# Other constants for a kernel's build-time scheduler: urgencies of loads and attention, a first chunk of eleven tiles, exponentials gathered in fours, loads expected at 290 GB/s

## The chip, the cores and the metric

The kernel runs on one core of a Trainium2 chip. The time is the device time of that core in microseconds. Engines are named as in the profile: PE (TensorE), DVE (VectorE), ACT (ScalarE), POOL (GpSimd), and SP (SyncE), whose queue issues most of the DMAs.

## The reference

Three stages follow each other. Attention works on 4 batches of 8 heads, 576 tokens, head dimension 64: one softmax attention over means of four neighbouring tokens (`out_d`, repeated four times along the sequence), plus one that sees only keys less than four positions away. The two sums make a matrix of 2304 tokens x 512. Then come two dense blocks, with all of their weights in float64, which the kernel reads as 64-bit words:

```python
def _moe_ref(x, w_in, w_out):            # 2304 x 512, d_ff 2048
    h = x @ w_in
    g = h * np.cos(h)
    return (g @ w_out).astype(np.float32)

def _moe2_ref(x, w1, w2, w3, w_out):     # 2304 x 512, d_ff 1024
    a = x @ w1
    b = x @ w2
    h = a * b @ w3
    return (h @ w_out).astype(np.float32)
```

## The kernel before

**Weights.** Each 128x512 block of 64-bit words is loaded on SP's queue into a tile `raw` and turned into float32 by `w_job` (L308): ACT writes `t`, DVE shifts `t` (TENSOR_SCALAR), DVE joins both words (SCALAR_TENSOR_TENSOR). For `wi` (of `w_in`) and `wo` (of `w_out`) ACT then copies a rounded part and POOL subtracts it, so that each product is made of three matmuls of rounded parts (`mm3`). `w3` and `w4` (of the second block's `w3` and `w_out`) are multiplied with each other beforehand, in plain float32: `w5_job` (L733) makes 64 calls into four banks `ps_w`, in two rounds of 32. `w5_out_job` (L755) copies each of the four banks to a slot of kind `t` and stores it from ACT's queue (`w_sc<-w`); the slot counts as free only when the store has landed (`give_stored`, L239), and six slots of kind `t` serve everything that is converted.

**Attention.** A pair of heads (`pair_job`, L446) goes through scores `ps_s`, exponentials `sd`, a division, transposes `ps_t`, copies `ptp`, product `ps_p`, and ACT's copy `up`. A unit of 192 tokens (`unit_job`, L571) goes through `ps_sb`, `sc`, the exponential, sums `bsum`, POOL's product, transposes `ps_tb` with copies `pt` on ACT, and `ps_av`; DVE adds both parts to `xb`, ACT and POOL split it into `xs`. Two units make a chunk of 384 tokens, and six chunks make the whole. Pooled values take `vr` and `vd` on DVE.

**First dense block.** A step is one chunk by one of 32 tiles of 128 hidden units. `h_job` (L826) makes 12 matmuls into a bank `ps_h`; `chain_job` (L806) makes g = h cos(h) of it: `turns` on ACT, `c` on DVE, Sin and Square on ACT, `c` on DVE (this gives the bank back), then `g` on ACT and POOL. `y_job` (L853) makes the 12 matmuls into four banks `ps_y` that stay open for the chunk; at a hand-over to other tokens `y_out_job` (L877) copies them to `yt` on ACT and stores them. `plan` (L783) sets the order: chunk 0 runs over the first HALF tiles, chunk 1 over the same tiles, then both over the rest, then the other chunks over all 32. The sums of the first part go to `part_sc`. The second dense block (`ps_ab`, `ps_o`) follows at 582 us.

**What sets the order.** All of these are jobs of a scheduler that runs while the program is built. Its own clock goes by `cost` (L83) and by the delays in LATENCY (L62). Whenever an engine is free by that clock, the ready job with the lowest urgency gets it (`run`, L264), so constants shift whole rows of instructions on every engine; on the chip each engine then works its row off in that order and waits only on semaphores. Urgencies of loads and attention come from A0, A1 and the U_ constants (L55 to L58, used in L1074 to L1115): the jobs of chunk 0 have A0 plus U_QK, U_PAIR, U_POOL or U_UNIT, the converters of `w4` and `w3` -1 to 7, those of the second round of `w3` 8 + U_W3 and on, those of `wi` and `wo` 16 + U_WI or U_WO plus the tile's first step, each step of h and its chain 16 plus its number. Copies of `ps_w` have -20, those of `ps_y` -10. SLACK (L53) is how long a slot must have been free before a load may go into it. `exps` (L552) holds exponentials until TOGETHER of them wait, or the first has waited for PATIENCE ns, or ACT's table is that of Exp anyway, so that it is swapped with Sin less often. While PE has nothing to do before the first h step, `warm_up` fills in matmuls on zeros (`ps_z`, or into `ps_w`).

Of the kernel before, what the change touches and what calls it, by code (L numbers as in the profile page):

```python
# [13 lines left out]
I64 = mybir.dt.int64  # L14
# [29 lines left out]
NH = N2 // 2  # L44
NCH2 = NT // N2
NQ = 7
HALF = 10
SCALE = 1.0 / math.sqrt(D)
TWO_PI = 2.0 * math.pi
LAG = 3  # L50
WARM = 256
EARLY_WARM, RISEN, REST = 3000.0, 10000.0, 130.0
FIRST, SLACK = 3000.0, 1000.0  # L53
TOGETHER, PATIENCE = 3, 6000.0
A0, A1 = 11, 4  # L55

U_QK, U_PAIR, U_POOL, U_UNIT = -13, -12, -11.5, -8
U_WI, U_WO, U_W3 = -4, -0.5, -1  # L58
OUT_BANKS = (4, 5, 6, 7, 2, 3)
EARLY = 2  # L60
BIAS, BANDS = 2, 4
LATENCY = {"pe": 200, "se": 140, "ve": 130, "ge": 150, "sy": 2000}  # L62


def band_of(u, w):
# [5 lines left out]
def fused_kernel(ctx: ExitStack, tc: tile.TileContext, qk_block, v_block, qk_pool, v_pool,  # L71
# [8 lines left out]
    def size(a):  # L80
        return math.prod(a.shape[1:])

    def cost(name, op, out, ins, func):  # L83
        n = max(size(a) for a in [out] + ins)
        if name == "ve":
            shared = n > 64 and ends["ge"] > max(now[0], ends["ve"])
            if op.startswith("tensor_scalar") and len(ins) == 1:
                return 90 + n * (1.5 if shared else 0.65)
            both = len(ins) == 2 and n > 64 and not any(a.tensor.name.startswith("ps_") for a in ins)
            return 75 + n * (2.2 if both and shared else 1.17 if both else 1.04)  # L90
        if name == "se":
            load = 1283 if func in (AF.Exp, AF.Sin) and func != table[0] else 0
            table[0] = func if load else table[0]
            return (60 if ins[0].tensor.name.startswith("ps_") else 100) + n / 1.2 + load
        if name == "ge":
            return 160 + (1.7 if any(0 in [step for step, _ in a.ap] for a in ins) else 2.3) * n
        if name == "sy":
            return max(450, n * out.shape[0] * (8 if out.dtype == I64 else 4) / 310)
        n = size(out)
        if op == "transpose":  # L100
            return 70
        if ins[0].dtype == F32R:
            return 12.5 + n / 2.4
        return (4 if ins[0].shape[0] == P else 2) * max(35, n / 2.4)

    def visible(a):

        end, by = written.get(a.tensor.name, (0.0, "pe"))
        return end + LATENCY[by]

    class Engine:
# [3 lines left out]
        def __getattr__(self, op):  # L115
            call = getattr(self.engine, op)

            def issue(*args, **kw):
                also = kw.get("accum_out")
                aps = [a for a in list(kw.values()) + list(args) if isinstance(a, bass.AP) and a is not also]  # L120
                out = kw["out"] if "out" in kw else args[0]
                if op == "dma_start" and self.name != "sy":
                    ends[self.name] = max(now[0], ends[self.name]) + 70
                    written[out.tensor.name] = ends[self.name] + cost("sy", op, out, [out], None), "sy"
                    return call(*args, **kw)
                first = next(k for k, a in enumerate(aps) if a is out)
                ins = aps[:first] + aps[first + 1:]
                end = ends[self.name] = max(now[0], ends[self.name]) + cost(self.name, op, out, ins, kw.get("func")) + (0 if also is None else 183)
                for a in (out, out if also is None else also):
                    written[a.tensor.name] = end, self.name  # L130
                return call(*args, **kw)  # L131

            return issue

    ve, se, pe, ge, sy = (Engine(*e) for e in (("ve", nc.vector), ("se", nc.scalar), ("pe", nc.tensor), ("ge", nc.gpsimd), ("sy", nc.sync)))
# [71 lines left out]
    def until(cond):  # L207
        while not cond():
            yield "until", cond
# [26 lines left out]
    def give(name, slot, engine):  # L236
        free[name].append((ends[engine] + LATENCY[engine], slot))

# [7 lines left out]
    def reached(key, n):  # L246
        return lambda: done.get(key, 0) >= n
# [535 lines left out]
    def plan():  # L783

        f = 0
        while f < F1:
            if f >= HALF:
                yield from until(lambda: reached(("x", 1), UPC)() or ("wi", f) in w_t)
# [260 lines left out]
    with tc.manual_schedule():  # L1049
# [20 lines left out]
        first, seen = {}, []  # L1070
        first.update({i: HALF if i == 1 else F1 * i for i in range(NC1)})
        first.update({("f", f): f if f < HALF else f + HALF for f in range(F1)})

        def attention(i, at):  # L1074

            for b in sorted({(UPC * i + m) // UPB for m in range(UPC)} - set(seen)):
                seen.append(b)
                if b < EARLY:
                    for m in range(UPB):
                        Job(at + U_QK + 0.5 * m, unit_qk_job(UPB * b + m))  # L1080
                for p in range(KC):
                    Job(at + U_PAIR + 2 * p, pair_job(b, p))
                    Job(at + U_POOL + 2 * p, pool_v_job(b, p))
            for m in range(UPC):
                Job(at + U_UNIT + 3 * m, unit_job(UPC * i + m))
# [24 lines left out]
        for i in range(2, NC1):  # L1110
            run(reached("h", first[i - 1] + 1 if i > 2 else first[0] + HALF + 1))
            attention(i, W5 + first[i])
# [71 lines left out]
```

## Time and profile before

| | |
|---|---|
| median of 3 runs | 866.26 us (864.69 to 868.79) |
| the profiled execution | 865.21 us |
| its span in the trace | 863.4 us |
| PE busy | 842.7 us, 98% |
| DVE, ACT, POOL busy | 503.3, 446.9, 366.6 us (58%, 52%, 42%) |
| HBM traffic | 89.49 MB read, 27.79 MB written |
| the chain that ended last | PE 86%, DVE 5%, DMA 4%, ACT 2% of the span |

PE is nearly always busy, so a term of time is either a stretch in which PE waits, or one in which it runs at half clock: the clock granted is half in two short stretches, one that ends 16.3 us after the start and one near 112 to 118.6 us. Nearly every operation is recorded by one helper line, L131 (DMA issues of ACT: L125), so the tiles' names tell the operations apart.

### The profile page before, as it was taken

The page shows a single profiled execution, that of the slowest core. Times are in us where ns is not written, and L with a number is a line of the kernel's source. Part 1 is how long each engine was busy: PE and PEld are TensorE (multiplying, and loading weights), DVE is VectorE, ACT ScalarE, POOL GpSimd, SP SyncE. Part 2 cuts the span into 40 slices and gives each one's busy share as a digit, 9 for nine tenths or more (in the row PEclk, how much of TensorE's full clock was granted, in tenths as well). Part 3 has the DMA queues.
Part 4 walks back from the last instruction along what each step waited for, and adds up shares of the span by engine and source line. Part 5 has one row for each costly group of instructions (what it writes and reads, how often), then busy time and mean ns, then how long its engine had stood idle before and what let it go on. Part 6 is the DMA issues. An engine that isn't in the chain of part 4 may idle for free.

```text
span 863.4 us, 14938 instructions
## 1 busy us (share of the span) xinstructions
PE 842.7 (98%) x5627; PEld 760.4 (88%) x5627; DVE 503.3 (58%) x897; ACT 446.9 (52%) x908; POOL 366.6 (42%) x330
## 2 busy tenths in 40 slices
PE   8999989999999999999999999999999999999998
PEld 6454579989999899999999999999999899989997
DVE  5988687985537883787356434715335633364332
ACT  2655689876766775677667556651113311231111
POOL 0013677746442445245425344524334633363333
PEclk8999989999999999999999999999999999999999
DMA  9989982131446523555161329782000500021001
GB/s 277 294 252 349 311 251 81 59 114 49 143 145 202 172 87 110 177 163 158 56 212 52 110 101 352 278 296 72 24 25 25 171 25 25 13 71 52 25 25 73
DMA packets 59479, 118.24 MB, mean 137 GB/s; under 512 B 18232, under 2 KB 25400, under 8 KB 59408
## 3 DMA queue, kind: packets, MB, share of 16 engines
q1 hardware_dynamic: 53040, 108.76, 39.4%
q10 hardware_dynamic: 6368, 8.54, 2.8%
q8 instruction: 44, 0.72, 0.4%
q14 instruction: 27, 0.22, 0.1%
HBM read 89.49 MB, written 27.79 MB: 136 GB/s over the span
## 4 chain that ended last, share of the span: by engine, by line
PE 86%; DVE 5%; DMA 4%; ACT 2%; issue 1%; SPq 1%; POOL 0%; ACTq 0%; DVEq 0%; POOLq 0%
PE ps_h L131 21%; PE ps_y L131 21%; PE ps_ab L131 20%; PE ps_o L131 12%; PE ps_w L131 5%; DVE t L131 2%; PE ps_av L131 2%; PE ps_tb L131 2%; DMA w_sc<-w 1%; DMA raw<-w3t 1%; PE ps_p L131 1%; DMA kb<-qk_block 1%; PE ps_s L131 1%; PE ps_sb L131 1%; PE ps_t L131 1%
## 5 line engine op out<-in xcount | busy, mean ns | idle before, releaser
L131 PE MATMUL ps_h<-xs,wi 128*128 128x384 f32 x1152 | 225.3, 340 | 2.1 <-ACT up L131 1.8
L131 PE MATMUL ps_y<-g,wo 128*128 128x384 f32 x1152 | 222.5, 337 | 1.6 <-ACT yt L131 1.6
L131 PEld LDWEIGHTS ps_h<-xs,wi 128*128 128x128 f32 x1152 | 200.8, 189 | 6.6 <-issue 2.8
L131 PEld LDWEIGHTS ps_y<-g,wo 128*128 128x128 f32 x1152 | 199.6, 188 | 4.3 <-ACT yt L131 2.3
L131 PE MATMUL ps_ab<-y,w 128*128 128x384 f32 x1008 | 186.2, 337 | 1.7 <-ACT v L131 1.5
L131 PEld LDWEIGHTS ps_ab<-y,w 128*128 128x128 f32 x1008 | 176.7, 188 | 8.5 <-ACT v L131 2.1
L131 DVE TENSOR_TENSOR v<-v,ps_ab 128x384 f32<-128x384 f32 x168 | 90.7, 552 | 142.2 <-ACT w L131 73.5
L131 POOL TENSOR_TENSOR g<-c,g 128x384 fp32r<-128x384 f32 x96 | 104.2, 1086 | 158.2 <-ACT g L131 131.2
L131 ACT ACTIVATE c<-c 128x384 f32<-128x384 f32 x192 | 100.6, 524 | 35.0 <-DVE c L131 32.3
L131 POOL TENSOR_TENSOR v<-v 128x384 f32<-128x384 f32 x48 | 50.3, 1047 | 146.3 <-DVE v L131 145.5
L131 PE MATMUL ps_o<-w,m 128*128 128x512 f32 x432 | 107.8, 392 | 0.0
L131 ACT CAST m<-v 128x384 fp32r<-128x384 f32 x48 | 24.7, 515 | 157.0 <-POOL v L131 157.0
L131 DVE SCALAR_TENSOR_TENSOR c<-turns,ps_h 128x384 f32<-128x384 int32 x96 | 52.8, 550 | 72.6 <-ACT turns L131 65.3
L131 PEld LDWEIGHTS ps_o<-w,m 128*128 128x128 f32 x432 | 80.3, 188 | 13.8
L131 DVE SCALAR_TENSOR_TENSOR c<-c,ps_h 128x384 f32<-128x384 f32 x96 | 52.7, 549 | 56.3 <-ACT c L131 55.9
L131 ACT CAST g<-c 128x384 fp32r<-128x384 f32 x96 | 49.1, 512 | 44.1 <-DVE c L131 40.0
L131 ACT ACTIVATE turns<-ps_h 128x384 int32<-128x384 f32 x96 | 46.8, 488 | 40.5 <-PE ps_h L131 39.5
L131 PE MATMUL ps_w<-w,w 128*128 128x512 f32 x128 | 59.4, 604 | 0.4 <-DVE w L131 0.4
L131 ACT ACTIVATE t<-raw 128x512 f32<-128x512 f32 x72 | 47.3, 670 | 22.3 <-DMA raw<-w3t 8.5
L131 DVE TENSOR_SCALAR t<-t 128x512 int32<-128x512 int32 x72 | 46.5, 661 | 14.8 <-ACT t L131 14.6
L131 POOL TENSOR_TENSOR sc<-sc,bsum 128x840 f32<-128x840 f32 x12 | 22.6, 1884 | 64.8 <-DVE bsum L131 44.4
L131 POOL TENSOR_TENSOR m<-v,m 128x384 fp32r<-128x384 f32 x48 | 48.3, 1025 | 2.5 <-ACT m L131 2.5
(86 smaller groups left out, 871.5 us busy)
## 6 DMA issues: line engine op xcount, KB each, us to landing
w_sc<-w SPq DMA_DIRECT2D x56, 256.0 KB
w<-w_sc SPq DMA_DIRECT2D x28, 512.0 KB
raw<-w SPq DMA_DIRECT2D x24, 512.0 KB
raw<-w3t SPq DMA_DIRECT2D x16, 512.0 KB
raw<-w_in SPq DMA_DIRECT2D x16, 512.0 KB
raw<-w_out SPq DMA_DIRECT2D x16, 512.0 KB
w5r<-w_sc SPq DMA_DIRECT2D x24, 256.0 KB
kb<-qk_block SPq DMA_DIRECT2D x12, 408.0 KB
```

Source lines behind the costliest of these rows:

```text
L131: return call(*args, **kw)
```

## The change

Only constants change; no instruction's kind or size does. The counts of instructions of DVE, ACT, POOL and SP stay, PE has 18 matmuls on zeros more, and ACT swaps its table 20 times in both programs.

```diff
-HALF = 10
+HALF = 11
-FIRST, SLACK = 3000.0, 1000.0
-TOGETHER, PATIENCE = 3, 6000.0
-A0, A1 = 11, 4
-
-U_QK, U_PAIR, U_POOL, U_UNIT = -13, -12, -11.5, -8
-U_WI, U_WO, U_W3 = -4, -0.5, -1
+FIRST, SLACK = 3000.0, 850.0
+TOGETHER, PATIENCE = 4, 6750.0
+A0, A1 = 6.0, 6
+
+U_QK, U_PAIR, U_POOL, U_UNIT = -13, -13, -10.5, -8.5
+U_WI, U_WO, U_W3 = -6, -1.0, -2.5
-LATENCY = {"pe": 200, "se": 140, "ve": 130, "ge": 150, "sy": 2000}
+LATENCY = {"pe": 200, "se": 140, "ve": 130, "ge": 150, "sy": 2450}
-            return max(450, n * out.shape[0] * (8 if out.dtype == I64 else 4) / 310)
+            return max(450, n * out.shape[0] * (8 if out.dtype == I64 else 4) / 290)
```

**DVE in the opening**, up to the first pair of weights that PE's first `ps_w` call needs (before: `w4_296` and `w3_321`; after: `w4_323` and `w3_346`). Before:

```order
L131 TENSOR_REDUCE bmax_144<-ps_sb_182 128x6
L131 TENSOR_SCALAR t_281<-t_281 128x512
L131 TENSOR_REDUCE nm_136<-ps_s_286 72x2
L131 TENSOR_REDUCE nm_136<-ps_s_287 72x2
L131 SCALAR_TENSOR_TENSOR w4_296<-raw_258,t_281 128x512
L131 TENSOR_SCALAR nm_136<-nm_136 72x4
L131 TENSOR_TENSOR vr_264<-vr_264 72x2x256
L131 TENSOR_SCALAR t_310<-t_310 128x512
L131 TENSOR_TENSOR vd_266<-vr_264 72x256
L131 SCALAR_TENSOR_TENSOR w3_321<-raw_273,t_310 128x512
```

After; between the row of `sc` and the first row here stand now `vr`, `bmax`, two rows of `nm`, `vd`, and the scaling of `nm`:

```order
L131 TENSOR_REDUCE bsum_142<-sc_140 128x12
L131 TENSOR_SCALAR t_301<-t_301 128x512
L131 TENSOR_SCALAR bsum_142<-bsum_142 128x12
L131 RECIPROCAL bsum_142<-bsum_142 128x12
L131 SCALAR_TENSOR_TENSOR w4_323<-raw_267,t_301 128x512
L131 TENSOR_SCALAR sums_135<-sums_135 72x4
L131 RECIPROCAL sums_135<-sums_135 72x4
L131 TENSOR_SCALAR t_320<-t_320 128x512
L131 TENSOR_TENSOR sd_134<-sd_134,sums_135 72x576
L131 TENSOR_REDUCE nm_139<-ps_s_333 72x2
L131 TENSOR_REDUCE nm_139<-ps_s_334 72x2
L131 SCALAR_TENSOR_TENSOR w3_346<-raw_277,t_320 128x512
```

The sums `bsum`, their division, the division of the first `sd` and the second pair's `nm` have moved ahead of the first pair of converted weights. On SP's queue the load of `vr` now stands ahead of the first `w4`, that of unit 0's `vb` ahead of the fourth.

**PE from the first h step on** (`ps_h`). Before:

```order
L131 MATMUL ps_h<-xs,wi 128x384 x6
L131 MATMUL ps_t<-ident,sd 72x72 x8
L131 MATMUL ps_h<-xs,wi 128x384 x6
L131 MATMUL ps_p<-ptp,vd 64x144 x4
L131 MATMUL ps_s<-qkd 72x144 x4
L131 MATMUL ps_h<-xs,wi 128x384 x12
L131 MATMUL ps_tb<-ident,sc 70x128 x12
L131 MATMUL ps_av<-pt,vb 64x64 x16
L131 MATMUL ps_h<-xs,wi 128x384 x21
```

After:

```order
L131 MATMUL ps_h<-xs,wi 128x384 x3
L131 MATMUL ps_t<-ident,sd 72x72 x8
L131 MATMUL ps_h<-xs,wi 128x384 x21
L131 MATMUL ps_p<-ptp,vd 64x144 x4
L131 MATMUL ps_h<-xs,wi 128x384 x12
L131 MATMUL ps_tb<-ident,sc 70x128 x4
L131 MATMUL ps_av<-pt,vb 64x64 x16
L131 MATMUL ps_h<-xs,wi 128x384 x12
L131 MATMUL ps_y_1447<-g,wo 128x384 x3
```

Before, a `ps_s` group, 12 `ps_tb` transposes and a `ps_av` group follow the second h step; now three h steps stand ahead of four transposes. Ahead of the first h step PE now does two groups each of `ps_t` and `ps_p` more, and 20 `ps_tb` and 24 `ps_av` calls more.

**ACT in the same place**, around the copies `w5` of the second round of `ps_w` and their stores. Before:

```order
L131 COPY ptp_1036<-ps_t_1137 72x288
L131 ACTIVATE t_1150<-raw_1079 128x512
L131 ACTIVATE sc_859<-sc_859 128x840
L131 ACTIVATE up_1002<-ps_p_1156 128x144
L131 ACTIVATE turns_1160<-ps_h_946 128x384
L131 CAST wo_1168<-t_1084 128x512
L131 ACTIVATE t_1176<-raw_1089 128x512
L131 ACTIVATE t_1177<-raw_1101 128x512
L131 ACTIVATE sd_990,sums_991<-ps_s_1169,nm_992 72x144 x2
L131 ACTIVATE sd_990,sums_991<-ps_s_1170,nm_992 72x144 x2
L131 ACT_TABLE_LOAD
L131 ACTIVATE c_1186<-c_1186 128x384
```

After; the first two stores (`w5_1258`, `w5_1267`) stand seven and five rows ahead of this piece:

```order
L131 COPY w5_1321<-ps_w2_922 128x512
L131 COPY ptp_1306<-ps_t_1318 72x288
L125 DMA w5_sc6_65<-w5_1321 128x512
L131 COPY ptp_1306<-ps_t_1319 72x288
L131 CAST wi_1287<-t_1211 128x512
L131 COPY w5_1349<-ps_w3_937 128x512
L131 ACTIVATE turns_1346<-ps_h_1001 128x384
L125 DMA w5_sc7_66<-w5_1349 128x512
L131 CAST wo_1312<-t_1237 128x512
L131 ACTIVATE t_1351<-raw_1220 128x512
L131 ACT_TABLE_LOAD
L131 ACTIVATE c_1359<-c_1359 128x384
```

Before, `t_1150`, which waits for the slot of the first store, stands behind the `ptp` copies and ahead of five exponentials and the swap of the table. Now the exponentials stand ahead of the stores, `w5_1349` waits for the first store's slot, and `t_1351` for the second's, with the swap behind it.

**ACT at the first hand-over**, where the four `ps_y` banks are copied (`yt`). Before:

```order
L131 ACTIVATE yt_1964<-ps_y0_1300 128x384
L131 CAST wo_1966<-t_1857 128x512
L125 DMA part_sc_58<-yt_1964 128x384
L131 CAST wi_1974<-t_1866 128x512
L131 ACTIVATE c_1972<-c_1972 128x384 x2
L131 ACTIVATE yt_2006<-ps_y1_1367 128x384
L125 DMA part_sc_58<-yt_2006 128x384
L131 ACTIVATE turns_2011<-ps_h_1986 128x384
L131 ACTIVATE yt_2021<-ps_y2_1396 128x384
L131 ACTIVATE yt_2028<-ps_y3_1405 128x384
```

After:

```order
L131 ACTIVATE yt_2027<-ps_y0_1447 128x384
L131 ACTIVATE yt_2035<-ps_y1_1477 128x384
L125 DMA part_sc_58<-yt_2027 128x384
L131 ACTIVATE yt_2041<-ps_y2_1488 128x384
L125 DMA part_sc_58<-yt_2035 128x384
L131 ACTIVATE c_2031<-c_2031 128x384
L125 DMA part_sc_58<-yt_2041 128x384
L131 CAST wo_2029<-t_1992 128x512
L131 ACTIVATE c_2031<-c_2031 128x384
L131 CAST wo_2068<-t_2011 128x512
L131 ACTIVATE yt_2102<-ps_y3_1505 128x384
```

Three of the four copies now stand in the first four rows, and the fourth stands last. PE's row has, between the last old `ps_y` group and the first new one, 12 h matmuls before, and 9 h matmuls, 24 of `ps_sb` and 3 h matmuls after.

## Rows read from the trace of the kernel before

**Rows 1.** The page: busy us of each engine; share of the chain of waits.
```profile
PE 842.7 (98%) x5627; PEld 760.4 (88%) x5627; DVE 503.3 (58%) x897; ACT 446.9 (52%) x908; POOL 366.6 (42%) x330
...
PE 86%; DVE 5%; DMA 4%; ACT 2%; issue 1%; SPq 1%; POOL 0%; ACTq 0%; DVEq 0%; POOLq 0%
```

**Rows 2.** PE in order of time, opening: start, us, instructions [idle before <-releaser].
```profile
22.59 3.70 PE L131 MATMUL ps_w<-w,w 128*128 128x512 f32 x8
...
30.93 1.13 PE L131 MATMUL ps_w<-w,w 128*128 128x512 f32 x2 [0.42 <-DVE w L131]
```

**Rows 3.** DVE in order of time, the same stretch.
```profile
18.35 0.81 DVE L131 TENSOR_REDUCE nm<-ps_s 72x2 f32<-72x288 f32 x2
...
19.75 0.68 DVE L131 TENSOR_TENSOR vr<-vr 72x512 f32<-72x512 f32 x1
...
21.17 0.68 DVE L131 SCALAR_TENSOR_TENSOR w<-raw,t 128x512 int32<-128x512 int32 x1
...
22.23 0.99 DVE L131 TENSOR_REDUCE bsum<-sc 128x12 f32<-128x840 f32 x1
23.14 0.74 DVE L131 TENSOR_TENSOR sd<-sd,sums 72x576 f32<-72x576 f32 x1
...
27.70 1.81 DVE L131 TENSOR_SCALAR t<-t 128x512 int32<-128x512 int32 x1
```

**Rows 4.** PE in order of time, the wait at 70 us.
```profile
70.20 0.71 PE L131 MATMUL ps_s<-qkd 64*72 64x144 f32 x8 [1.09 <-DVE qkd L131]
```

**Rows 5.** Busy us by stretch: PE, PEld, DVE, ACT, POOL, PEclk, DMA share, GB/s.
```profile
100.00:120.00 20.00, 15.27 (x110) 12.95 (x109) 12.07 (x23) 14.93 (x35) 9.69 (x8) 0.83 0.99 303
104.00:112.00 8.00, 4.21 (x28) 3.13 (x28) 6.21 (x16) 7.21 (x18) 1.58 (x2) 0.99 0.94 310
112.00:118.60 6.60, 5.92 (x45) 5.36 (x46) 5.78 (x7) 4.82 (x11) 5.05 (x4) 0.50 1.02 301
280.00:300.00 20.00, 17.91 (x166) 16.16 (x159) 17.07 (x30) 13.95 (x26) 8.02 (x9) 1.00 0.49 150
```

**Rows 6.** PE in order of time, from the first h step on.
```profile
102.98 1.00 PE L131 MATMUL ps_p<-ptp,vd 72*64 72x144 f32 x8 [0.26 <-ACT ptp L131]
...
106.45 2.36 PE L131 MATMUL ps_h<-xs,wi 128*128 128x384 f32 x12 [1.82 <-ACT up L131]
109.22 1.30 PE L131 MATMUL ps_tb<-ident,sc 128*70 128x128 f32 x8 [0.42 <-issue]
112.68 1.07 PE L131 MATMUL ps_tb<-ident,sc 128*70 128x128 f32 x4 [2.16 <-ACT pt L131]
```

**Rows 7.** ACT and its DMA issues in order of time, the same stretch.
```profile
98.21 0.33 ACTq L125 DMA_DIRECT2D w_sc<-w  x1
...
104.76 0.66 ACT L131 ACTIVATE t<-raw 128x512 f32<-128x512 f32 x1 [1.54 <-DMA w_sc<-w]
...
109.86 1.28 ACT L131 ACT_TABLE_LOAD   x1
111.15 0.52 ACT L131 ACTIVATE c<-c 128x384 f32<-128x384 f32 x1
```

**Rows 8.** Chain of waits in order of time, from 60 us: the first store's landing.
```profile
57.25 5.24 DMA w_sc<-w
```

**Rows 9.** PE in order of time, hand-over of the first chunk.
```profile
169.93 2.37 PE L131 MATMUL ps_h<-xs,wi 128*128 128x384 f32 x12 [0.26 <-DVE c L131]
...
173.95 0.79 PE L131 MATMUL ps_y<-g,wo 128*128 128x384 f32 x3 [1.13 <-ACT yt L131]
175.22 1.31 PE L131 MATMUL ps_y<-g,wo 128*128 128x384 f32 x6 [0.48 <-ACT yt L131]
```

**Rows 10.** PE in order of time, 281 to 287 us.
```profile
281.19 2.24 PE L131 MATMUL ps_y<-g,wo 128*128 128x384 f32 x12
283.27 0.69 PE L131 MATMUL ps_h<-xs,wi 128*128 128x384 f32 x3
285.44 0.42 PE L131 MATMUL ps_t<-ident,sd 72*72 72x72 f32 x4 [1.48 <-DVE sc L131]
```

## Prediction

> **What bounds the kernel now.** The page first: PE is busy for 842.7 of 863.4 us and carries 86% of the chain of waits [rows 1]. No instruction's size changes, so the time moves only by what PE waits, by its granted clock, and by the matmuls on zeros before the first h step. So I read PE in order of time, and then, where a row carries idle time, the engine named as releaser, and what that engine did before. The table by stretches shows how uneven the waits are: 100 to 120 us holds 4.73 us of idle PE, 280 to 300 us 2.09 us [rows 5]. Beside the former lies the one stretch behind the opening at half clock: in 104 to 112 us PE is busy for only 4.21 of 8 us, and in 112 to 118.6 us the clock is 0.50, that is 1.2 instead of 2.4 GHz [rows 5]. The reader is to see there that one cause, ACT held up, was paid twice.
>
> The sum is made against the profiled execution, 865.21 us, of which the span is 863.4; it lies 1.05 us below the median of 866.26.
>
> **Opening: DVE converts later.** Before, `w3_321` ends at 21.85 us (21.17 + 0.68) [rows 3] and PE starts `ps_w` at 22.59 [rows 2]. By the order on DVE, `bsum`, the division of the first `sd`, and the second pair's `nm` now stand ahead of the first pair of weights: start to start 0.91 (22.23 to 23.14), about 0.7 for `sd`, 0.7 for `nm`, and three or four small operations, together 2.7 us [rows 3]. The load of `vr` ahead of the first weights costs about 1 us more if the DMAs bound this (295 KB at the 300 GB/s seen elsewhere [rows 5]). Further, the shift of `t` now comes while POOL multiplies `sc`; where that happened before, it took 1.81 us [rows 3] instead of some 0.4, so 0 to 1.4 us more. `ps_w` then starts 3.1 to 4.4 us later. Before, PE lost 0.42 us at 30.93 [rows 2] and about 0.8 us to two matmuls on zeros there; after has 16 of these ahead of the first `ps_w` (they fill a wait, and cost nothing by themselves) and three later. I take a lag of 3.2 us, ends 2 and 4.5. It is not all kept. At 70.20 PE waits 1.09 us for `qkd`, whose data come by DMA [rows 4]; a PE that arrives later finds them there, while that transfer moves little. So **+2.1 us**, ends 0.9 and 3.4. Between 31 and 99 us PE has no other idle time to give, so nothing else takes the lag back.
>
> **Attention moved ahead of the first h step.** PE does about 7.5 us more of it before that step, so the step begins near 109 us instead of 99.5. The same matmuls are missing later: nothing in the sum. It gives the weights of w_in and w_out more time to arrive; that hides the extra tile of HALF, whose two weight loads (1 MB) were due by the same queue anyway: nothing.
>
> **The stall behind the first h step.** Before: idle 0.26 + 1.82 + 0.42 + 2.16 = 4.66 us [rows 6]. ACT stood before `t` until the first store `w_sc<-w`, issued at 98.21, had landed at 104.74; then came exponentials, and 1.28 us of table loading at 109.86, ahead of the `pt` copies that PE waited for [rows 7]. Half clock cost as much again: 5.92 us busy at 0.50 [rows 5], half of which, 2.96, would have been free. Together 7.6 us.
>
> After, by the order: the exponentials stand ahead of the stores, and PE has three h steps before the transposes that need the bank of the first. Let T be the first h step's start. A step is 2.08 us (281.19 to 283.27 [rows 10]), so PE reaches these transposes at T + 7.1 (36 matmuls of h, 6.24, plus `ps_t` and `ps_p`, 0.85). On ACT the first store is issued about T - 3.1 (three `ps_w` calls of 0.9, `ps_p` and `ps_tb` come after its bank). A store landed 5.24 us [rows 8] to 6.53 us [rows 7] after its issue: T + 2.1 to T + 3.4. From there the chain is `w5` 0.6, `turns` 0.5, `wo` 0.6, `t` 0.7, the table 1.28, `c` 0.5, `up` 0.3, `c` 0.5 and DVE 0.5, and the bank comes back at T + 7.6 to T + 8.9. PE so waits 0.5 to 1.8 us, and perhaps 0.8 elsewhere in the stretch: 1.3 taken, ends 0.5 and 2.6. The clock should hold: at 285.44 PE waited 1.48 us in one piece, and the clock in that stretch was 1.00 [rows 10, 5]. So 7.6 - 1.3, **-6.3 us**; ends -7.1, and -2.0 if it is idle for 2.6 and then pays 3.0 at half clock.
>
> The skill bears on the swap of tables. In the row, `ACT_TABLE_LOAD` takes 1.28 us from 109.86, and Sin begins at 111.15, directly behind it [rows 7]. The Trainium skill, ScalarE: Activation LUTs, "What ACT_TABLE_LOAD costs", adds a drain of about 1.38 us to a load of about 1.28, 2.66 us a switch; no drain is seen in this row. By the page's figure the chain above would be 1.4 us longer and this term about -4.9 us; the sum goes by the row.
>
> **Hand-over of the first chunk.** Before, PE waits 0.26 + 1.13 + 0.48 = 1.87 us, mostly for the `yt` copies [rows 9], between which ACT does `wi`, `wo` and both operations on `c`. After, three copies stand in front, so the first new groups have their banks, and 4.3 us of PE work (9 h, 24 `ps_sb`, 3 h, 9 y) stand between the last old group and the one that needs the fourth copy, which comes after about 4.2 us of ACT. I take 0.5 us left: **-1.4 us**, ends -1.9 and 0.
>
> **The rest.** From about 185 us on the rows of both orders are nearly alike, shifted by a tile. Gathering in fours saves no table load: 20 in both. One pair of swaps falls in a later place; on the Sin chain with no cover it is 2 x 1.28, beside PE's work nothing. Waits like the one at 285.44, 2.09 us in its stretch [rows 5, 10], can go or come anew. I take **+0.5 us**, ends -3 and +4. SLACK, LATENCY and 290 GB/s act only through the order, so they have no term of their own.
>
> **Sum:** 2.1 - 6.3 - 1.4 + 0.5 = -5.1, so 865.2 - 5.1 = 860.1 us.
>
> **The rivals.**
>
> *The stall only moves (same).* ACT still waits for landed stores, now twice (`w5_1349`, `t_1351`), with the table load behind. For it: stores took up to 6.53 us at a time when the DMAs were 94% busy or more [rows 5, 7]. Against it: three h steps as cover, where there were two with gaps. If idle is 2.6 us and the clock falls once more, this term is -2.0, the sum 2.1 - 2.0 - 0.5 + 0.5 = +0.1: 865.3 us. On the clock the Trainium skill, TensorE: Matmul & The Clock Gate, "What's actually happening", says that the throttled state is the default and that activity releases it, so a stretch with gaps may throttle again as at 112 us. It is a condition of this rival.
>
> *Late hand-overs starve (slower).* By the order, the work that PE has between a chunk's last `ps_av` and the first h step on that chunk shrinks from about 6.7 to 2.6 us for the third hand-over of chunks and from 2.6 to 2.1 for the one before. Behind `ps_av` stand DVE's sum, ACT's and POOL's split: some 2 us. If exponentials held for a fourth, or a longer patience (6.75 us), bring the last unit more than 2 us later, PE stands still there, and a long gap costs the clock too, as in 104 to 118.6 us: up to 4.7 + 3.0 us a place. Two such places at 5.5 each make 860.1 + 11 = 871 us. Against it: no hand-over of before shows more than 1.9 us, and PE has y groups in hand there. It decides once ACT's exponentials come over 2 us later than now in relation to PE.
>
> *More waits go (faster still).* If the opening's lag is 2 us, of which 1.1 is taken back, the stall ends at 0.5, and the wait at 285.44 vanishes too (-2.1): 0.9 - 7.1 - 1.9 - 2.1 = -10.2: 855 us.
>
> **How the numbers follow.** The forecast, 857 to 863.5 us: 0.45. Faster still, 851 to 857: 0.17. The stall moves, 863.5 to 868: 0.24. Starved hand-overs, 868 to 874: 0.14. The range leaves out about half of the slower rival, and a little of the fastest: 853 to 869 us. This kernel's runs can tell about 0.5% (4.3 us) from no change, so faster is below 861.9: 0.17 and 0.37 of the forecast's, 0.54; slower, above 870.6, 0.12; same 0.34.
>
> **What would show it.** Right: `ps_w` starts at 25.5 to 27 us; no wait at `ps_s` <- `qkd` near 73; the first `ps_h` near 109; behind it idle PE of 0.5 to 2.6 us and clock 1.00 throughout 100 to 130 us; less than 1 us for `yt`. Wrong: half clock in that stretch, or an idle PE of more than 1 us at the first h of a late chunk (`xs` as releaser, on ACT or POOL), or a lag in the opening above 5 us.

## The result and the profile after

| | before | after |
|---|---|---|
| median | 867.05 us (864.69 to 868.79) | 856.90 us (856.30 to 857.15) |
| ratio, 95% interval | | 0.9884 (0.9858 to 0.9910) |
| span of the profiled execution | 863.4 us | 854.9 us |

The changed kernel is 1.2% faster: 8.5 us in the two traces, 10 us in the medians. One word on the kernel as described above: the first dense block has 16 tiles of 128 hidden units, not 32 (96 steps in all); nothing in the sums uses that count.

The page of after, engines and chain, in the columns of [rows 1]:

```profile
PE 840.2 (98%) x5645; PEld 757.8 (89%) x5645; DVE 500.4 (59%) x897; ACT 443.9 (52%) x908; POOL 366.0 (43%) x330
...
PE 86%; DMA 6%; DVE 4%; ACT 2%; issue 1%; POOL 0%; SPq 0%; ACTq 0%; DVEq 0%; POOLq 0%
```

PE's busy time has hardly changed; 2.5 us less of it, and 6 us less idle time. Where they went is read best by **equal work**: each matmul of the trace counts its usual start-to-start time at full clock (173 ns for h and y, 429 for half a `ps_w` call, and so on; those on zeros count nothing), and the two traces are compared where the same sum has been started. The counting of the small matmuls moves the points by up to 2 us and the differences by a few tenths. A wait that shows in a row as idle time, one that hides in a longer matmul, and half clock are all in it.

| useful PE work started, us | 20 | 70 | 90 | 130 | 150 | 260 | 380 | 400 | 520 | 780 |
|---|---|---|---|---|---|---|---|---|---|---|
| time in before, us | 41.0 | 96.9 | 126.6 | 167.9 | 191.3 | 307.2 | 434.4 | 455.1 | 576.7 | 841.4 |
| after minus before | +2.7 | +2.2 | -3.8 | -3.5 | -6.6 | -9.0 | -7.6 | -8.3 | -7.5 | -8.7 |

So 2.7 us are lost in the opening (2.2 of it left at 97 us), 6.0 gained around the first h steps, 3.1 at the first hand-over, 2.4 between 191 and 307 us; then the difference wanders within 1.5 us. In the same columns as [rows 5], after:

```profile
100.00:120.00 20.00, 18.40 (x135) 12.74 (x132) 12.88 (x23) 14.86 (x35) 11.08 (x9) 1.00 0.86 277
160.00:180.00 20.00, 20.00 (x159) 19.66 (x158) 18.91 (x29) 14.58 (x30) 15.80 (x12) 1.00 0.51 177
280.00:300.00 20.00, 20.00 (x207) 18.12 (x198) 16.09 (x31) 14.05 (x28) 8.13 (x8) 1.00 0.69 207
```

The clock is 1.00 in 100 to 120 us, where it was 0.83, and idle time there is 1.6 instead of 4.7 us; the other two stretches have none left. The opening on PE, beside [rows 2]:

```profile
25.01 1.98 PE L131 MATMUL ps_w<-w,w 128*128 128x512 f32 x4 [1.69 <-DVE w L131]
```

And on DVE and POOL, beside [rows 3]:

```profile
20.88 1.56 DVE L131 TENSOR_SCALAR sums<-sums 72x4 f32<-72x4 f32 x1
...
22.57 0.39 DVE L131 TENSOR_SCALAR t<-t 128x512 int32<-128x512 int32 x1
...
24.28 0.68 DVE L131 SCALAR_TENSOR_TENSOR w<-raw,t 128x512 int32<-128x512 int32 x1
```
```profile
20.57 1.84 POOL L131 TENSOR_TENSOR sc<-sc,bsum 128x840 f32<-128x840 f32 x1 [19.39 <-ACT sd L131]
```

Ahead of the second of the two weights, `w` at 24.28, stands more than was there; and a scaling of `sums`, four numbers a partition, took 1.56 us, while POOL multiplied `sc`. From the first h step on, PE and ACT, beside [rows 6] and [rows 7]:

```profile
109.75 1.08 PE L131 MATMUL ps_h<-xs,wi 128*128 128x384 f32 x3
...
116.19 0.71 PE L131 MATMUL ps_p<-ptp,vd 72*64 72x144 f32 x8 [1.13 <-DVE vd L131]
...
119.66 0.63 PE L131 MATMUL ps_tb<-ident,sc 128*70 128x128 f32 x4 [0.47 <-DVE c L131]
```
```profile
107.73 0.33 ACTq L125 DMA_DIRECT2D w_sc<-w  x1
...
108.22 0.33 ACTq L125 DMA_DIRECT2D w_sc<-w  x1
...
114.14 0.59 ACT L131 COPY w<-ps_w 128x512 f32<-128x512 f32 x1 [1.68 <-DMA w_sc<-w]
...
115.91 0.68 ACT L131 ACTIVATE t<-raw 128x512 f32<-128x512 f32 x1 [0.17 <-DMA w_sc<-w]
116.60 1.28 ACT L131 ACT_TABLE_LOAD   x1
```

ACT still waits for both stores, 1.68 and 0.17 us, and loads its table right behind. The first store took 6.4 us from 107.73 to its landing at 114.1, the second 7.6 us from 108.22 to its landing at 115.83. But this now falls beside three h steps, and PE waits 1.13 + 0.47 us. The first of these is new: `ps_p` waits for `vd`, and DVE had `vd` in its row behind `c`, which waited for ACT's `turns`, which stood behind the wait for the store.

### The profile page after: what moved, and what is told of

It is laid out like the page before. It is cut to its first block, busy times and chain, and to the rows that moved or that the text cites. A ratio compares the mean times of both kernels' runs of the same rounds, so it can differ in the third digit from the quotient of the medians.

```text
span 854.9 us, 14975 instructions
## 1 busy us (share of the span) xinstructions
PE 840.2 (98%) x5645; PEld 757.8 (89%) x5645; DVE 500.4 (59%) x897; ACT 443.9 (52%) x908; POOL 366.0 (43%) x330
## 4 chain that ended last, share of the span: by engine, by line
PE 86%; DMA 6%; DVE 4%; ACT 2%; issue 1%; POOL 0%; SPq 0%; ACTq 0%; DVEq 0%; POOLq 0%
PE ps_y L131 22%; PE ps_h L131 21%; PE ps_ab L131 19%; PE ps_o L131 12%; PE ps_w L131 5%; PE ps_av L131 2%; DMA w_sc<-w 2%; PE ps_tb L131 2%; DMA kb<-qk_block 1%; DMA raw<-w_in 1%; PE ps_p L131 1%; PE ps_sb L131 1%; PE ps_s L131 1%; PE ps_t L131 1%; DMA y_sc<-yt 1%
## 5 line engine op out<-in xcount | busy, mean ns | idle before, releaser
L131 PE MATMUL ps_h<-xs,wi 128*128 128x384 f32 x1152 | 219.5, 337 | 0.7 <-ACT ptp L131 0.5
L131 PE MATMUL ps_w<-w,w 128*128 128x512 f32 x128 | 61.6, 608 | 1.7 <-DVE w L131 1.7
L131 POOL TENSOR_TENSOR xs<-xb,xs 128x512 fp32r<-128x512 f32 (+1 forms) x24 | 27.1, 1128 | 50.8 <-ACT xs L131 47.1
```

## The experiments

All lags below are read as in the table above: time minus that of before, at equal work.

| run | 20 | 70 | 90 | 130 | 150 | 260 | 380 | 400 | 520 | 780 | ratio to before (95%) |
|---|---|---|---|---|---|---|---|---|---|---|---|
| after | +2.7 | +2.2 | -3.8 | -3.5 | -6.6 | -9.0 | -7.6 | -8.3 | -7.5 | -8.7 | 0.9884 (0.9858-0.9910) |
| e1 before, fours | -1.4 | -1.2 | -1.2 | +0.3 | +0.2 | -0.1 | +0.4 | -0.1 | +0.7 | +1.1 | 0.9993 (0.9971-1.0015) |
| e2 before, own slots | -0.7 | -1.9 | -4.6 | -4.3 | -4.4 | -5.6 | -3.6 | -4.1 | -2.3 | -2.3 | 0.9958 (0.9933-0.9982) |
| e3 before, eleven | -1.3 | +1.2 | +3.7 | +5.9 | +3.1 | +2.1 | +2.4 | +2.4 | +3.3 | +3.8 | 1.0026 (1.0007-1.0044) |
| e4 after, threes | +3.4 | +2.7 | -3.8 | -3.5 | -6.0 | -7.2 | -5.1 | +13.7 | +13.7 | +12.3 | 1.0128 (1.0102-1.0153) |
| e5 before, attention early | +1.6 | +5.0 | +2.8 | +3.8 | +5.4 | +4.7 | +4.2 | +16.0 | +16.0 | +16.5 | 1.0183 (1.0167-1.0200) |
| e6 before, POOL zeros | -1.0 | -2.1 | -3.1 | -3.1 | -6.1 | -6.1 | -5.8 | -5.3 | -5.4 | -4.9 | 0.9972 (0.9951-0.9993) |
| e7 after, own slots | +4.1 | +3.0 | -4.7 | -3.3 | -4.2 | -6.2 | -6.2 | +4.6 | +4.6 | +2.8 | 1.0029 (1.0009-1.0049) |
| e8 after, A0 11 | +0.5 | -0.8 | -4.7 | -3.5 | -6.6 | -8.4 | -6.9 | -7.7 | -7.4 | -8.2 | 0.9888 (0.9862-0.9913) |
| e9 after, threes, one by one | +3.0 | +1.9 | -5.9 | -5.6 | -8.1 | -8.4 | -7.8 | -7.9 | -7.4 | -3.7 | 0.9944 (0.9924-0.9964) |
| e10 after, weights later | +3.4 | +2.3 | -3.7 | -3.0 | -1.3 | -2.8 | -2.1 | +15.0 | +14.9 | +13.5 | 1.0169 (1.0133-1.0205) |
| e11 after, A0 11, one by one | -0.5 | -1.7 | -7.6 | -5.3 | -8.4 | -9.8 | -6.9 | -7.4 | -6.8 | -7.6 | 0.9924 (0.9897-0.9950) |
| e12 after, ten | +2.9 | +2.4 | +0.4 | -0.4 | +0.4 | -0.6 | +0.6 | +0.1 | +0.1 | -1.0 | 0.9967 (0.9953-0.9981) |

The lags of a row are those of one execution. e1, e2, e3 and e6 have the order of before up to 20 us of work, and lie 0.7 to 1.4 us off there: so much is scatter from one execution to the next, and only steps over 1 us between neighbouring columns are read. e6's traced execution is the fastest of its ten (860.28 against a median of 862.20 us), so its last columns say more than its ratio does.

**e1: gathering alone.**

```diff
-TOGETHER, PATIENCE = 3, 6000.0
+TOGETHER, PATIENCE = 4, 6750.0
```

> The kernel before with TOGETHER 4 and PATIENCE 6750 alone. In its order the opening and the rows around the first h step are word for word those of before; at the first hand-over the yt copies stand as in the changed kernel (two, a store, a third, a store, the fourth). Theory (each stall has its own cause in the order of ACT): span up to 160 us as before, with idle PE of 4 to 5 us and half clock behind the first h step; at the hand-over idle PE of under 0.6 instead of 1.87 us; 2 to 4 us faster. Rival (the hand-over was gained by where the program stands against its loads, through eleven tiles and the urgencies): 1.5 to 2 us of idle remain there and the time is within 1.5 us of before.

The stall behind the first h step stayed, as expected. The `yt` copies now stood together, and yet the hand-over was as dear as before (lag +0.3 to +0.2). PE at the hand-over:

```profile
170.65 2.37 PE L131 MATMUL ps_h<-xs,wi 128*128 128x384 f32 x12 [0.72 <-DVE c L131]
...
176.18 0.79 PE L131 MATMUL ps_h<-xs,wi 128*128 128x384 f32 x3 [1.08 <-DVE c L131]
```

The waits for `yt` [rows 9] are gone, and waits for DVE's `c`, 0.72 and 1.08 us, stand in their place. So the compact `yt` row is not what gained the time; the theory behind that term of the prediction fell.

**e6: DVE without POOL's subtractions.** The kernel before, instruction for instruction, but for:

```diff
-    yield from on("ge", lambda: ge.tensor_tensor(out=w[:, 1, :], in0=t..., in1=w[:, 0, :]..., op=ALU.subtract), w)
+    yield from on("ge", lambda: ge.memset(w[:, 1, :].bitcast(F32), 0.0), w)
```

> The kernel before, with every instruction in its place, but POOL writes zeros into the second part of wi and wo instead of subtracting (the rounding rest of both weights is left out of the products). It asks whether the 1.87 us of the first hand-over are DVE held up by POOL. Theory (they are): DVE's shifts of t beside it fall from 2.2 to 2.5 us to 0.4 to 0.8 each, DVE is busy for under 18 of 20 us in 160 to 180, the idle PE in 168 to 178 us falls below 0.6 us, and the kernel is 1.5 to 4 us faster. Rival (ACT's row, with the yt copies between conversions, sets it): over 1.2 us of idle stay there although DVE is quicker; at most 1 us faster.

Before and e6 in the columns of [rows 5], and the wait of ACT in before ahead of its first `yt`:

```profile
160.00:180.00 20.00, 18.05 (x141) 16.62 (x140) 20.00 (x26) 15.02 (x31) 16.03 (x12) 1.00 0.27 94
```
```profile
160.00:180.00 20.00, 20.00 (x158) 19.44 (x157) 18.94 (x31) 14.86 (x32) 9.12 (x11) 1.00 0.43 146
```
```profile
169.96 0.51 ACT L131 CAST g<-c 128x384 fp32r<-128x384 f32 x1 [1.23 <-DVE c L131]
```

PE's idle time in 160 to 180 us is gone, and 3.0 us with it (lag -3.1 to -6.1), although ACT's row is that of before with conversions between the `yt` copies. DVE is still busy for 18.94 us, not under 18, and single shifts still take up to 2.06 us, so the theory's sizes were off. In before DVE has no idle time in these 20 us, so it was not late because it waited for something that POOL delivers; what e6 took away is time that DVE's operations lose beside POOL's: its 512-wide joins took 0.68 us each in e6 and 1.04 in before. So at the hand-over of before **PE waits for DVE, and DVE is slow beside POOL**; that ACT's `yt` is named in [rows 9] is what came last: ACT itself had waited for DVE's `c`. In before DVE starts 7 of the 512-wide shifts in 160 to 180 us, 8.4 us together, in after 5 with 4.2 us: two had begun before 160 us, and the others took 0.8 us each instead of 1.2.

**e10: the weights' urgencies undone.**

```diff
-U_WI, U_WO, U_W3 = -6, -1.0, -2.5
+U_WI, U_WO, U_W3 = -4, -0.5, -1
```

> The changed kernel with the old urgencies of the weights, U_WI -4, U_WO -0.5, U_W3 -1. Theory (the first hand-over was gained because weights are converted earlier and more evenly, so that DVE is not full there): at 160 to 180 us DVE is busy for over 19.5 of 20 us again, and PE has 1.2 us or more of idle in 165 to 182 us. Rival (the order of yt, or the eleventh tile, made it): idle under 0.6 us there. In its order the fifth chunk's last ps_av stands at the end of the chunk before, as in the other runs that lost 9 to 14 us at 420 to 450 us, so that much is lost there by either: 8 to 16 us slower than the changed kernel in all.

```profile
162.23 2.36 PE L131 MATMUL ps_h<-xs,wi 128*128 128x384 f32 x12 [1.03 <-DVE c L131]
...
169.65 0.33 PE L131 MATMUL ps_sb<-kb,qb 64*64 64x70 f32 x2 [2.36 <-DVE sc L131]
```

Between 130 and 150 us of work the lag goes from -3.0 to -1.3, where after gains 3.1, so the hand-over's gain is gone without these three numbers. All of the waits name DVE (`c`, `sc`), and the clock is at half (1.2 of 2.4 GHz) from 170.2 to 173.6 us, behind the longest of them. But DVE was busy for 19.04 us in 160 to 180 us, not over 19.5, and for 18.91 in after, so how full DVE is does not tell the two apart. That the weights come earlier in after is shown (POOL ends its eleventh `wi` at 140 instead of 145 us); that nothing else in the order changed at the hand-over is not.

**e2: the stores' slots.**

```diff
-        slot = yield from take("t")
+        slot = yield from take("w")
...
-        give_stored("t", slot, w5_sc[f])
+        give_stored("w", slot, w5_sc[f])
```

> The kernel before, but the copies of ps_w are kept in slots of the weights' kind until their stores have landed, not in slots that converted weights wait for; exponentials and the table load still stand ahead of the pt copies. Theory (ACT held by the store's landing starves PE): between 100 and 116 us idle PE falls from 4.66 us to 1 to 2.5 us and the clock stays at its full level; 3 to 6 us faster. Rival (the exponentials and the table load ahead of pt are enough to make the stall): idle PE stays at 4 us or more with half clock, and the time within 1.5 us of before.

```profile
104.73 1.30 PE L131 MATMUL ps_tb<-ident,sc 128*70 128x128 f32 x8 [0.34 <-POOL wo L131]
108.19 1.07 PE L131 MATMUL ps_tb<-ident,sc 128*70 128x128 f32 x4 [2.16 <-ACT pt L131]
```

The 1.82 us before `ps_h` [rows 6] are gone, since ACT no longer waits for a store; the 2.16 us for `pt`, behind exponentials and a table load, stay to the hundredth, and the clock is again 0.83 in 100 to 120 us. Both theories had half: the store and the exponentials are paid one after the other. e2's lag moves by 2.7 us here, that of after by 6.0.

**e3 and e12: the eleventh tile.** Each with one line, e3 HALF 11 in the kernel before, e12 HALF 10 in the changed one:

```diff
-HALF = 10
+HALF = 11
```

> The kernel before with HALF 11 alone. In its order the opening is that of before, while three and a half h steps and a whole y step stand ahead of the 12 transposes, and the yt copies at the hand-over are compact. Theory (cover by h steps behind the first one removes the stall, and attention need not be moved ahead for it): first ps_w at 22.6 us as before, idle PE of at most 2.5 us and full clock in 98 to 118 us, under 0.6 us at the hand-over; 6 to 10 us faster than before, as fast as the changed kernel or faster by up to 2 us. Rival (the gain comes from attention moved ahead of the first h step by the urgencies): idle of 4 us and half clock remain behind the first h step; at most 3 us faster.

> The changed kernel with HALF 10 again. Its order has the opening of the changed kernel, three h steps and more between the first h step and the bank that they wait for, and late chunks with 7 to 20 us of h and y steps behind their last ps_av. Theory (the eleventh tile has no price of its own; the stall behind the first h step is gone by the urgencies of attention together with the expected delays of DMA, which move the stores away from it): first ps_w at 24 to 26 us, idle PE of at most 2 us and full clock behind the first h step, within 3 us of the changed kernel in all. Rival (eleven tiles are what makes room): 4 us of idle or half clock are back behind the first h step, or more than 1.5 us of idle at the hand-over, and the kernel is 4 us or more slower than the changed one.

In e3 the order had three h steps ahead of the `ps_tb` transposes, and the stall moved one row up, to the transposes `ps_t` of a pair behind the first h step; in e12 PE has only one h step (12 matmuls) ahead of its `ps_tb`. PE in both, then the engines of e12 by stretch, then ACT and POOL of e12:

```profile
107.93 0.69 PE L131 MATMUL ps_t<-ident,sd 72*72 72x72 f32 x4 [4.30 <-DVE sc L131]
109.33 1.33 PE L131 MATMUL ps_h<-xs,wi 128*128 128x384 f32 x3 [0.71 <-DVE sc L131]
```
```profile
112.41 1.21 PE L131 MATMUL ps_p<-ptp,vd 72*64 72x144 f32 x8 [0.99 <-ACT ptp L131]
...
116.58 0.63 PE L131 MATMUL ps_tb<-ident,sc 128*70 128x128 f32 x4 [1.73 <-ACT up L131]
```
```profile
110.00:116.60 6.60, 3.84 (x22) 2.53 (x20) 0.29 (x1) 4.08 (x9) 5.17 (x4) 1.00 0.59 208
116.60:123.40 6.80, 6.80 (x50) 6.49 (x51) 2.28 (x4) 4.57 (x8) 2.96 (x2) 0.56 0.88 323
```
```profile
111.48 0.59 ACT L131 COPY w<-ps_w 128x512 f32<-128x512 f32 x1 [4.19 <-POOL wo L131]
```
```profile
104.82 6.62 POOL L131 TENSOR_TENSOR wo<-t,wo 128x512 fp32r<-128x512 f32 x1 [1.63 <-ACT wo L131]
```

e12 is 4.2 us behind after at 90 us of work, with half clock once more, 7.0 at 150, and 7.5 in the whole trace. So eleven tiles do make room in after, and do harm in before: the rival of both runs was nearer. The chain in e12 is not that of [rows 7], though: ACT's copy of `ps_w` stands 4.19 us before a slot that POOL gives back, not before a store, and POOL's subtraction for `wo` lasts 6.6 us there. HALF enters the urgencies of chunk 1's attention and of the weights beyond it, and it puts the first hand-over one tile later.

At the hand-over the eleventh tile counts in both kernels. e3 gains 2.8 us between 130 and 150 us of work (+5.9 to +3.1), though DVE is as full as in before:

```profile
160.00:180.00 20.00, 19.74 (x209) 18.87 (x209) 20.00 (x26) 15.48 (x31) 15.34 (x13) 1.00 0.38 129
```

e12 gains nothing there (-0.4 to +0.4; PE waits 1.92 us for `c` at 171.20 us). So a DVE without idle time does not by itself hold PE. The gain of after needs the eleventh tile (e12) and the weights' urgencies (e10); how they share it was not separated.

**e5 and e8: attention's urgencies.**

```diff
 # e5, in the kernel before
-A0, A1 = 11, 4
-U_QK, U_PAIR, U_POOL, U_UNIT = -13, -12, -11.5, -8
+A0, A1 = 6.0, 6
+U_QK, U_PAIR, U_POOL, U_UNIT = -13, -13, -10.5, -8.5
 # e8, in the changed kernel
-A0, A1 = 6.0, 6
+A0, A1 = 11, 6
```

> The kernel before with the new A0, A1, U_QK, U_PAIR, U_POOL and U_UNIT alone. In its order the attention of the first chunks stands ahead of the weights, as in the changed kernel, and four h steps follow the first one before any transposes. Theory (these urgencies carry both the cost in the opening and the gain behind the first h step): first ps_w 2 to 4 us later than before, no wait at 70 us, idle PE of at most 1.5 us and full clock behind the first h step; 3 to 5 us ahead of before at 160 us, and faster by 2 to 8 us in all. Rival (the weights' urgencies or the delays of DMA are what removed the stall): half clock and 4 us of idle PE stay.

> The changed kernel with A0 11 again (attention of the first chunk as far behind as before). Its order has 13 matmuls on zeros fewer ahead of the first ps_w, and four h steps with little between them after the first. Theory (A0 is what delays the opening): first ps_w within 1 us of before's 22.6 us; 1 to 3 us ahead of the changed kernel at 100 us; full clock behind the first h step. Rival (the order of vr and of the sums in front of DVE's conversions stays, so the lag stays): first ps_w at 24.5 us or later. In all 3 us slower to 3 us faster than the changed kernel.

Alone, the urgencies lose 5 us by 97 us, have the stall and half clock behind the first h step again, and then fall over a late hand-over (below). PE and ACT of e5:

```profile
115.45 5.77 PE L131 MATMUL ps_h<-xs,wi 128*128 128x384 f32 x30
...
127.34 4.21 PE L131 MATMUL ps_h<-xs,wi 128*128 128x384 f32 x12 [4.26 <-DVE xb L131]
```
```profile
118.79 0.59 ACT L131 COPY w<-ps_w 128x512 f32<-128x512 f32 x1 [2.58 <-DMA w_sc<-w]
...
125.11 0.66 ACT L131 ACTIVATE t<-raw 128x512 f32<-128x512 f32 x1 [2.78 <-DMA w_sc<-w]
125.79 1.28 ACT L131 ACT_TABLE_LOAD   x1
```

Thirty-six matmuls of h stood as cover, and it was not enough, since all of `w5` came late: ACT stood 2.58 and 2.78 us before stores. So cover and the place of the stores have to fit. In e8 `ps_w` starts at 22.86 us, the lag at 20 us of work is +0.5 instead of +2.7, and the time is that of after. So the opening's loss is A0's. But what it saves there is spent again: PE waits 1.54 + 0.93 + 0.78 us at the first h steps, the gain from 70 to 90 us of work is 3.9 instead of 6.0, and at 130 both lie at -3.5. In the whole A0 makes no difference that the runs show.

**e7: own slots in the changed kernel.** The edit of e2.

> The changed kernel with the copies of ps_w in slots of the weights' kind until their stores have landed. Theory (the last stall behind the first h step, 1.13 + 0.47 us, is still the store's landing, which holds ACT): idle PE of at most 0.5 us between 109 and 121 us; 1 to 1.6 us ahead of the changed kernel at 160 us; in all 0 to 3 us faster than it, if the later hand-overs keep their order. Rival (the table load and the row of DVE set it): 1 us or more of idle stays there.

The stall behind the first h step is gone altogether (PE busy for 20.00 of 20 us in 100 to 120 us; the lag at 90 us of work is -4.7 with an opening 1.4 us worse), so what was left of it in after was the store. But it does not last: PE then waits 1.84 us for POOL's `g` at 137.96 us (0.42 in after), and at 130 us of work the lag is -3.3 beside after's -3.5, not 1 to 1.6 us ahead. Other rows moved too: the first hand-over gains 0.9 instead of 3.1 us, and 11 us go at 430 to 447 us.

**e4 and e9: what the patience is worth.**

```diff
 # e4, in the changed kernel
-TOGETHER, PATIENCE = 4, 6750.0
+TOGETHER, PATIENCE = 3, 6000.0
 # e9: that, and in unit_job
-            qk_slots = yield from take("raw", 2)
+            qk_slots = yield from take("raw", 2) if u % 2 == 0 else one_by_one()   # take("raw") twice
```

> The changed kernel with TOGETHER 3 and PATIENCE 6000 again. Its order is that of the changed kernel up to and past the first hand-over. Theory (gathering in fours is worth nothing by itself, 20 table loads in all): within 2 us of the changed kernel, either way. Rival (the wait of 2.09 us at 283 us went because exponentials gather in fours): that wait is back, and the kernel is 2 to 3 us slower than the changed one.

> The kernel of the run with TOGETHER 3 and PATIENCE 6000 (span 875.6), and the second unit of each chunk from the third on takes its two slots of kind raw one after the other instead of both at once. By the order, its scores for the fifth chunk then stand 47 us earlier, behind those of the first unit, and PE has some 11 us of h and y steps left behind that chunk's last ps_av instead of none. Theory (the patience cost 20 us only because one unit stood without its two slots while single takers, the pooled keys and values, went by, so that the fifth chunk came late): the stretch of idle PE and half speed at 430 to 447 us goes; 11 to 17 us faster than that run, a span of 858 to 865. Rival (the shorter patience itself delays exponentials and starves PE): idle of 8 us or more stays near 430 us.

e4 was the surprise: with 2 us either way expected, it is 21 us slower than after. It is PATIENCE: with TOGETHER 3 and PATIENCE 6750 the program comes out row for row as after, so gathering in fours does nothing. Up to 260 us of work e4 keeps within 1.8 us of after, at 380 within 2.5; the rest goes at one place. PE of e4:

```profile
423.82 6.53 PE L131 MATMUL ps_y<-g,wo 128*128 128x384 f32 x36
437.43 2.78 PE L131 MATMUL ps_tb<-ident,sc 128*70 128x128 f32 x12 [7.07 <-POOL sc L131]
...
444.53 1.12 PE L131 MATMUL ps_av<-pt,vb 70*64 70x64 f32 x16 [2.42 <-DMA vb<-v_block]
447.69 7.08 PE L131 MATMUL ps_h<-xs,wi 128*128 128x384 f32 x24 [2.03 <-POOL xs L131]
```

Then SP's queue, e4 and after:

```profile
367.52 0.93 SPq L131 DMA_DIRECT2D qb<-qk_block  x2
373.85 0.37 SPq L131 DMA_DIRECT2D kb<-qk_block  x1
...
381.67 0.33 SPq L131 DMA_DIRECT2D qkr<-qk_pool  x1
382.10 0.35 SPq L131 DMA_DIRECT2D vr<-v_pool  x1
...
404.98 0.31 SPq L131 DMA_DIRECT2D vr<-v_pool  x1
...
412.26 1.85 SPq L131 DMA_DIRECT2D qb<-qk_block  x2
417.29 0.37 SPq L131 DMA_DIRECT2D kb<-qk_block  x1
```
```profile
357.15 0.93 SPq L131 DMA_DIRECT2D qb<-qk_block  x2
362.32 0.37 SPq L131 DMA_DIRECT2D kb<-qk_block  x1
...
369.61 0.94 SPq L131 DMA_DIRECT2D qb<-qk_block  x2
370.59 0.51 SPq L131 DMA_DIRECT2D kb<-qk_block  x1
...
377.28 0.33 SPq L131 DMA_DIRECT2D qkr<-qk_pool  x1
377.71 0.35 SPq L131 DMA_DIRECT2D vr<-v_pool  x1
```

In after the loads of the fifth chunk's two units (`qb`, `kb`) go out at 357 to 371 us, ahead of the next batch's pooled keys and values (`qkr`, `vr`). In e4 the second unit's go out at 412 to 417, behind all of those. The unit asks for both slots of kind `raw` at once, and `qkr` and `vr` take one each as it comes free. The unit is then 43 to 47 us late, and PE has done all other h and y steps when it needs it: 7.07 + 2.42 + 2.03 us of idle, and a mean clock of 0.72 in 420 to 450 us. e9 lets that unit take its slots one by one, with the shorter patience kept: the lag at 400 us of work is -7.9 instead of +13.7, and the stretch is full:

```profile
420.00:450.00 30.00, 29.78 (x259) 28.96 (x258) 18.67 (x34) 20.50 (x38) 11.98 (x12) 1.00 0.57 175
```

So at this place the patience had no price in itself. It moved the first claim, and one claim for two slots starved. e5, e7 and e10 show the same step, of 11 to 17 us, at the same place: in each the second unit's loads go out only at 403 to 420 us, behind `qkr` and `vr`, and the order has the fifth chunk's last `ps_av` where no h or y step of the chunk before is left, against 5.7 us of such work in after. e9 itself loses 6 us anew where the second dense block begins (lag -7.4 at 520, -1.9 at 540), with PE waiting for POOL's `y` and DVE's `v`; the cause is open.

**e11: a version meant to beat both.** A0 11, and slots one by one, in the changed kernel (the edits of e8 and e9, with the patience of after).

> A version meant to beat both: the changed kernel with A0 11 (opening of before) and slots of kind raw taken one by one by a chunk's second unit. Its order has 10 us of h and y steps behind the fifth chunk's last ps_av where the changed kernel has 5.7. Theory: up to 190 us as the run with A0 11 (6 us ahead of before), and waits of 320 to 480 us smaller by 0 to 3 us, since the late chunks come earlier: 853 to 857 us. Rival (nothing waits for those chunks in the changed kernel, so earlier loads only collide with others): 856 to 860 us.

It leads after by 3.8 us at 90 us of work and by 1.8 at 150, and has given it back by 380 (one wait of 2.3 us for POOL's `g` at 351 us): 0.9924 (0.9897 to 0.9950), no better than after. The rival was right. No version run here beats after beyond its interval.

**What the runs leave open.** Around the first h steps (70 to 90 us of work) after gains 6.0 us. With one group of constants put back at a time, the gain there is 6.5 (e4), 3.9 (e8), 6.0 (e10) and 2.0 (e12), so of these the eleventh tile matters most, and it does not do it alone (e3). SLACK, the delay of 2450 and the 290 GB/s also change the rows of the program, each by itself, and no run puts them back: their part is not shown.

## Why the prediction was right, and where it was off

The time lies in the range and on the forecast side. The gain is 8.5 us in the traces where 5.1 were summed. The median, 856.9 us, lies just below the forecast's band of 857 to 863.5, in that of "more waits go", which had 0.17.

- **Opening.** A lag of 3.2 us was forecast, `ps_w` at 25.5 to 27 us; it starts at 25.01, a little earlier, with a lag of 2.7. That +2.1 was left after the wait at 70 us and +2.2 measured is in part luck: a lag 0.5 us smaller lost 0.5 us, not 1.1. The wait for `qkd` is gone, but not because PE comes later: in e2 and e6, with the order of before, PE gets there 0.7 and 1.0 us earlier than in before, and does not wait either. POOL beside DVE did cost in the opening, but on the four numbers of `sums`, not on the shift.
- **First h steps.** -6.3 forecast, -6.0 measured (from +2.2 to -3.8). The chain named was right: both store waits, the table load and the late bank are in ACT's rows, and the clock held. The first store landed beyond the bounds, at T + 4.4 (114.1 less 109.75) instead of T + 2.1 to 3.4, since it was issued at T - 2.0 and took 6.4 us. The term's own rest was 1.6 us idle against 1.3 taken. What was not seen: PE's wait for `vd`, behind `c` in DVE's row, 1.13 us of the 1.6. And the extra tile of HALF, put at nothing, is worth 7.5 us in after: so much is e12 behind in the traces, in part here and in part at the hand-over.
- **Hand-over.** -1.4 forecast, -3.1 measured: the term that was mis-sized most, by two errors in one step. The price of before was added up from idle times in brackets, 1.87 us, where the same stretch costs 3 us at equal work (e6 gives 3.0 back). For example, three `ps_y` matmuls start at 172.14 us and the next ones at 173.95 [rows 9]: by the starts 1.29 us are lost there, and the bracket shows 1.13. The rest lies in rows that are longer than usual and show no idle time. And the cause was put on the row of `yt`, which e1 shows to be wrong. In before it was DVE, slow beside POOL (e6); in after it went with the eleventh tile and the earlier weights together.
- **The rest.** +0.5 forecast, -2.1 measured; the wait at 285 us [rows 10] is gone, which stood in the ends and in the fastest rival, not in the middle. It belongs to the one order of before: it stays in e6, which has that order, and in every other run, e1 and e2 among them, 1.2 to 2.9 us go between 240 and 250 us of work. So it takes no particular constant to move it.
- **The rivals.** "The stall only moves" is what e3, e5 and e12 do, with half clock and all; in e5 ACT stands before stores, as the rival had it, in e12 before POOL. "Late hand-overs starve" did not come in after, but it was not far: four of the twelve variants fall there, at 11 to 19 us instead of the 5.5 a place that I had put. Exponentials were not its root, though; in e4, where it was tried, the two slots were. The weight of 0.14 for it can't be judged by one draw, but its price was far too low.
- **The table load.** The Trainium skill, ScalarE: Activation LUTs, "What ACT_TABLE_LOAD costs", would have added a drain of about 1.38 us to each load. In after, the load at 116.60 takes 1.28 us and Sin starts at 117.90; no drain shows, and the measured -6.0 fits the sum without it.

## What to carry to other kernels

Where a scheduler lays out the program, its constants have no prices of their own: ask for the order, and look in it for cover (how many steps stand ahead of the first that needs the late thing) and for claims of several slots at once beside claims of one. Read the cost of a stall from start to start at equal work, and look at the engine that runs full as well as at the one that the last semaphore names. A place with a few microseconds of cover is a cliff for the next change, however good the time is now.

## What the runs showed of the hardware

- A DVE operation on four numbers a partition is not short beside POOL: the scaling of `sums` took 1.56 us in after's opening, while POOL multiplied `sc`; others of its kind in that trace took 0.16.
- The other way round, POOL's subtraction for `wo` in e12 lasted 6.6 us from 104.82 us, beside a DVE without idle time up to 110.3 us; 1.3 us is usual. That DVE held it was not tested.
- A store of 256 KB from ACT's queue took 5.2 and 6.5 us to land in before, 6.4 and 7.6 in after.
- One wait did not always bring the clock down. After kept 1.00 through 1.13 + 0.47 us of idle PE, and e8 through 1.54 + 0.93 + 0.78 us between 107 and 119 us; e12, idle for 0.99 + 1.73 us in the 6.6 us from 110, was at 0.56 on average in the 6.8 us behind that.
